# Tanh taken off by adding transfers instead of VectorE subtractions, in an fp32 attention and feed-forward kernel on Trainium2

## The chip, the cores and the metric

The kernel runs on one core of one Trainium2 chip. Five engines with queues of their own work side by side: TensorE (PE, with its weight loads shown apart as PEld), VectorE (DVE), ScalarE (ACT), GpSimd (POOL) and SyncE (SP). Each takes its instructions in the order in which they stand in its queue. Transfers are issued from SP's and POOL's queues and carried by 16 DMA engines. The time is the device's time of one execution in microseconds. The kernel before takes 674.85 us, the median of three runs (674.55 to 675.02).

## What is computed

The first part is a linear attention with a decay, over 4 batches, 8 heads, 768 positions and 64 channels. Its output, 3072 rows of 512, goes through a feed-forward part with 2048 hidden channels. All of it is float32.

```python
for b in range(nb):                       # blocks of 64 positions
    intra = np.einsum('bhic,bhjc->bhij', qb, kb) * Dmask[None]
    intra = np.einsum('bhij,bhjd->bhid', intra, vb)
    inter = np.einsum('bhid,bhde->bhie', qb * lam_pow[None], kv_state)
    out[:, :, sl] = intra + inter
    kv_state = lam_block[None, :, None, None] * kv_state + np.einsum('bhsd,bhse->bhde', kb_dec, vb)
...
h = x @ w_in                              # 3072x512 by 512x2048
g = h - np.tanh(h)
return (g @ w_out).astype(np.float32)     # 3072x2048 by 2048x512
```

## The kernel before

**Groups and units.** The rows are worked in six groups of 512 (`g` = 0 to 5), a group being 128 positions of each of the four batches. For a group the attention gives `xt`, 512 channels by 512 rows. The first product then makes the hidden blocks in four units (`u` = 0 to 3, 512 hidden channels each), and the second product makes the output rows out of them. Attention for group `g + 1` is run in pieces among the steps of group `g`.

**Seven products for eight.** From group 1 on, both products follow Strassen's scheme in Winograd's form: the operands are cut into quarters, seven products are made of sums of quarters, and their results are added into the four result blocks, called 11, 12, 21 and 22. `up(g, u, n)` (L424) issues product `n` of unit `u` of the first product; each is 8 matmuls of 128x256 in the trace. From group `GI` = 2 on, products 2 and 4 are themselves made in that way by `inner_steps` (L505), for all units at once and ahead of the rest, so that a unit is left with five: 6, 5, 1, 7 and 3. Product 1 of a unit is issued one unit early. Product 1, 6 and 7 gather in a PSUM bank y, products 5 and 3 in a bank z. There are two banks for y, which the units take in turn, and one for z: product 5 of a unit can't begin before VectorE has read z of the unit before.

**Result blocks.** `hidden(g, c)` (L418) is an SBUF tile for block `c` of all four units; there is one tile for each `c`, and the next group takes it over. After a product, `up` copies or adds its bank into these tiles: L446 adds y to block 11, L449 copies z to 22, L451 and L452 add y to 22 and 21, L461 copies y to 12, and L469 adds z to 12. `finish(c, src)` (L439) then takes the hyperbolic tangent off a block: ScalarE writes the tanh into a tile `th` (L441) and VectorE subtracts it from the block (L442). A block of a unit is 128 partitions by 512 float32, 256 KB. Behind the last of the four, L472 and L473 make two sums that the second product wants, S1 = 12 + 22 and then 12 = 11 - 12.

**Second product.** `down(g, 1)` reads block 11, `down(g, 2)` block 21; the others read 22, S1, 12 and differences made by `sums_once` (L626) and `sums_twice` (L676). Where a product of it is cut once more, `down_twice` (L684) issues it. The weight factors come from DRAM in pieces of 256 KB, in a fixed order, into a ring of seven tiles `wb` (`piece`, L594), issued from POOL. In group 2 the POOL queue also carries the making of the quarter factors: `load_quarters` (L571) loads them, `factors_twice` (L585) has VectorE make differences (L590) and stores them to DRAM (L591). Output tiles and some results between come from `otile` (L621), four buffers of 128x512 with the tag "o".

**Order.** The framework lays out each engine's queue: it takes the program's order as a priority and an estimate of when each instruction's inputs are ready, and puts in the semaphores. `keep_in_program_order` pins a few instructions. The loop that sets the order around the change:

```python
for n in (2, 6, 5, 7, 1, 4, 3) if g < GI else (1, 7, 3) if u == 0 else (6, 5, 1, 7, 3) if u + 1 < NU else (
        6, 5, 7, 1, 3):
    if n != 1:
        up(g, u, n)
    elif u + 1 < NU:
        up(g, u + 1, 1)
    else:
        every(down(g, 1))
```

The functions that the diff touches:

Of the kernel before, what the change touches and what calls it, by code (L numbers as in the profile page):

```python
# [13 lines left out]
AF = mybir.ActivationFunctionType  # L14
AL = mybir.AluOpType
# [8 lines left out]
def kernel(  # L24
# [32 lines left out]
    nc = tc.nc  # L57
# [8 lines left out]
    NU = DFF // 512  # L66
# [117 lines left out]
    GI = 2  # L184
# [224 lines left out]
    def product_bank(key, n):  # L409

        if n == 1:
            banks[key, "y"] = bank("y", "yb" if key[0] == "up" and key[2] % 2 else "ya", 1)
        if n in (2, 5):
            banks[key, "zw"[n == 2]] = bank("zw"[n == 2], "zw"[n == 2], 1)
        t = banks[key, {2: "w", 5: "z", 3: "z"}.get(n, "y")]
        return t.rearrange("q (m c) -> q m c", m=2), n in (1, 2, 5)

    def hidden(g, c):  # L418

        if (g, c) not in hid:  # L420
            hid[g, c] = gpool.tile([128, NU, 2, HB], F32, name=f"g{c}", tag=f"g{c}")
        return hid[g, c]

    def up(g, u, n):  # L424
        a, bname = FACT[n]
        wt = {"A11": w1[u][:, 0:2, 0], "A12": w1[u][:, 2:4, 0], "S3": w1[u][:, 0:2, 1], "A22": w1[u][:, 2:4, 1],
              "S1": ws[u][:, 0], "S2": ws[u][:, 1], "S4": ws[u][:, 2]}[a]
        x = xt[g][bname] if bname != "B11" else xt[g, 0][:, 0:2]
        key = ("up", g, u)
        t, first = product_bank(key, n)  # L430
        for m in range(2):
            for kt in range(2):
                nc.tensor.matmul(out=t[:, m, :], lhsT=wt[:, kt, ts(m, 128)], rhs=x[:, kt, :],  # L433
                                 start=first and m == 0 and kt == 0, stop=kt == 1, skip_group_check=True)

        def dst(c):
            return hidden(g, c)[:, u]

        def finish(c, src):  # L439
            th = work.tile([128, 2, HB], F32, name="th", tag="th")  # L440
            nc.scalar.activation(th, src, AF.Tanh)  # L441
            nc.vector.tensor_tensor(dst(c), src, th, op=AL.subtract)  # L442

        y, z, w = (banks[key, x].rearrange("q (m c) -> q m c", m=2) if (key, x) in banks else None for x in "yzw")
        if g >= GI and n == 1:
            nc.vector.tensor_tensor(dst(11), dst(11), y, op=AL.add)  # L446
            finish(11, dst(11))
        elif g >= GI and n == 5:
            nc.scalar.activation(dst(22), z, AF.Copy)  # L449
        elif g >= GI and n == 7:  # L450
            nc.vector.tensor_tensor(dst(22), dst(22), y, op=AL.add)  # L451
            nc.vector.tensor_tensor(dst(21), dst(21), y, op=AL.add)  # L452
            finish(22, dst(22))
            finish(21, dst(21))
        elif n == 1:
            nc.scalar.activation(dst(11), y, AF.Copy)
        elif n == 2:
            nc.vector.tensor_tensor(dst(11), dst(11), w, op=AL.add)
            finish(11, dst(11))
        elif n == 6:  # L460
            nc.scalar.activation(dst(12), y, AF.Copy)  # L461
        elif n == 7:
            nc.scalar.activation(dst(22), y, AF.Copy)
            nc.vector.tensor_tensor(dst(22), dst(22), z, op=AL.add)
            finish(22, dst(22))
        elif n == 4:
            finish(21, y)
        elif n == 3:
            nc.vector.tensor_tensor(dst(12), dst(12), z, op=AL.add)  # L469
            finish(12, dst(12))  # L470

            nc.vector.tensor_tensor(dst("S1"), dst(12), dst(22), op=AL.add)  # L472
            nc.vector.tensor_tensor(dst(12), dst(11), dst(12), op=AL.subtract)  # L473

# [144 lines left out]
    def otile(name):  # L621
        return opool.tile([128, 512], F32, name=name, tag="o")
# [219 lines left out]
    load_quarters(0)  # L842
    load_quarters(1)
    up(1, 0, 1)
    for g in range(1, NG):
        last = g == NG - 1
        p0, p1 = attention(g + 1) if not last else ([], [])
        for u in range(NU):
# [8 lines that stand above are left out]
                if g in turns:  # L857
                    made.append(n)
                    step = len(made) - turns[g][0]
                    for t, first in turns[g][1]:  # L860
                        if step == first:
                            if t > 1:
                                load_quarters(t)
                            making[t] = factors_twice(t)
                        if first <= step < first + 4:
                            next(making[t])
            if g == GI - 1:
                inner_weights(u)
            if not last and u > 1:
                run(p0[u - 2:u - 1])  # L870
# [65 lines left out]
```

## Time and profile before

| | |
|---|---|
| median of three runs | 674.85 us |
| span of the profiled execution | 672.3 us |
| granted TensorE clock | 1.00 throughout |
| stretch from 275 to 313 us (group 2, first product) | PE busy 37.46 us, DVE 32.36, ACT 12.80, POOL 14.24, DMA share 0.71 |
| stretch from 313 to 330 us (group 2, after it) | PE busy 17.00 us, DVE 17.00, POOL 5.54, DMA share 0.76 |
| tanh of a block (L441) | 630 ns on ScalarE |
| transfers issued from POOL | 541 to 757 ns on POOL each |
| software queue | 28976 packets, 96.49 MB, 45.4% of 16 engines' span |

The profile is of one execution. In its tables a line such as `L442 DVE TENSOR_TENSOR g<-g,th ... x76 | 51.9, 688 | 18.2` names line, engine, operation, what is written from what, and the count; then the busy time in us, the mean of one in ns, and the engine's idle time just before, with what ended it. In the timeline the first two columns are start and length in us, and a bracket holds the idle time before and its releaser. The stretches named by windows list busy time and count for each engine. In the rows of transfers the last number is the median time from issue to landing. The ends of matmuls are modelled, so starts are the better guide to TensorE's pace. A few matmul records can be missing from a trace.

### The profile page before, as it was taken

What the parts mean: (1) busy time and instruction counts of PE and PEld (TensorE: products, weight loads), DVE (VectorE), ACT (ScalarE), POOL (GpSimd) and SP (SyncE); (2) the same over time, 40 slices, a digit from 0 to 9 for tenths busy, and PEclk for the clock granted to TensorE, in tenths of its full rate; (3) what the DMA queues carried; (4) which work ended last, traced back from release to release, by engine and by line L of the source; (5) the groups of instructions that cost most, each with busy time, mean ns of one, the idle gap of its engine ahead of it and who ended that gap; (6) DMA issues with size and microseconds to landing.
All of it is one profiled execution on the core that took longest, in us unless ns stands there. A gap on an engine that the chain in (4) does not pass through costs nothing.

```text
span 672.3 us, 12869 instructions
## 1 busy us (share of the span) xinstructions
PE 661.7 (98%) x4824; PEld 576.3 (86%) x4824; DVE 481.3 (72%) x872; ACT 194.8 (29%) x373; POOL 200.5 (30%) x345
## 2 busy tenths in 40 slices
PE   8899999999999999999999999999999999999998
PEld 7688855558888999988999988899988899988997
DVE  4797867993887772499895379888358977357743
ACT  4564433423331111332112243112333112234110
POOL 0001424217332424244345201254300245400351
PEclk9999999999999999999999999999999999999999
DMA  9979799869855978587898632698730677610495
GB/s 209 222 205 236 238 268 255 290 147 271 249 148 139 243 191 210 127 239 236 228 285 253 176 80 58 150 292 255 225 73 13 160 236 220 217 35 1 126 289 164
DMA packets 162717, 128.80 MB, mean 192 GB/s; under 512 B 133856, under 2 KB 135008, under 8 KB 162656
## 3 DMA queue, kind: packets, MB, share of 16 engines
q0 software_dynamic: 28976, 96.49, 45.4%
q1 hardware_dynamic: 133536, 31.50, 23.6%
q8 instruction: 38, 0.62, 0.4%
q14 instruction: 23, 0.19, 0.1%
q10 hardware_dynamic: 144, 0.00, 0.0%
HBM read 103.55 MB, written 24.38 MB: 190 GB/s over the span
## 4 chain that ended last, share of the span: by engine, by line
PE 86%; issue 8%; DMA 2%; SPq 1%; POOL 1%; DVE 0%; ACT 0%; POOLq 0%; DVEq 0%; ACTq 0%
PE y L433 13%; PE y L695 11%; PE op L771 8%; PE z L433 8%; PE zw L695 8%; PE h L750 7%; PE w L642 4%; PE y L642 4%; PE y L517 4%; PE sp L327 3%; PE plain L642 3%; PE op L381 3%; PE z L517 2%; PE op L375 2%; PE kv L349 1%
## 5 line engine op out<-in xcount | busy, mean ns | idle before, releaser
L607 POOL DMA_DIRECT2D wb<-fine x147 | 79.4, 541 | 114.7 <-PE y L695 48.2
L610 POOL DMA_DIRECT2D wb<-factors x56 | 30.3, 543 | 155.2 <-PE y L642 97.3
L441 ACT ACTIVATE th<-g 128x512 f32<-128x512 f32 x76 | 47.6, 630 | 98.3 <-DVE g L446 33.2
L433 PE MATMUL y<-xt,w 128*128 128x256 f32 x320 | 74.0, 380 | 0.0
L433 PEld LDWEIGHTS y<-xt,w 128*128 128x128 f32 x320 | 59.9, 190 | 9.0 <-ACT g L521 0.9
L442 DVE TENSOR_TENSOR g<-g,th 128x512 f32<-128x512 f32 x76 | 51.9, 688 | 18.2 <-ACT th L441 18.1
L698 ACT ACTIVATE q<-y 128x128 f32<-128x128 f32 x84 | 23.3, 278 | 130.1 <-PE y L695 126.5
L750 PE MATMUL h<-xt,w 128*128 128x256 f32 x256 | 56.5, 381 | 2.0 <-DVE w L271 2.0
L771 PE MATMUL op<-wt,g 128*128 128x512 f32 x128 | 56.5, 595 | 0.0
L750 PEld LDWEIGHTS h<-xt,w 128*128 128x128 f32 x256 | 48.2, 190 | 9.2 <-DVE w L271 1.4
L695 PE MATMUL y<-wb,g 128*128 128x128 f32 x384 | 51.2, 278 | 0.0
L771 PEld LDWEIGHTS op<-wt,g 128*128 128x128 f32 x128 | 23.8, 190 | 27.7 <-issue 26.5
L695 PEld LDWEIGHTS y<-wb,g 128*128 128x128 f32 x384 | 46.4, 192 | 1.2 <-issue 0.3
L433 PE MATMUL z<-tt,ws 128*128 128x256 f32 x160 | 38.0, 380 | 0.0
L433 PE MATMUL z<-xt,ws 128*128 128x256 f32 x160 | 37.9, 380 | 0.0
L433 PE MATMUL y<-tt,ws 128*128 128x256 f32 x160 | 37.8, 379 | 0.0
L642 PE MATMUL y<-wb,g 128*128 128x256 f32 x160 | 35.6, 379 | 0.5 <-PE y L433 0.5
L198 POOL DMA_DIRECT2D raw<-in_moe_w_out_dram x16 | 8.9, 555 | 90.8 <-DVE g L758 52.3
L642 PE MATMUL w<-wb,g 128*128 128x256 f32 x160 | 35.8, 382 | 0.0
L331 DVE TENSOR_TENSOR ss<-sp,mask 128x512 f32<-128x512 f32 x48 | 30.9, 682 | 6.0 <-PE sp L327 6.0
L642 PEld LDWEIGHTS y<-wb,g 128*128 128x128 f32 x160 | 30.3, 190 | 5.0 <-PE y L433 0.9
L433 PEld LDWEIGHTS z<-xt,ws 128*128 128x128 f32 x160 | 30.3, 190 | 4.3 <-ACT g L449 0.2
(171 smaller groups left out, 1301.2 us busy)
## 6 DMA issues: line engine op xcount, KB each, us to landing
wb<-fine POOLq DMA_DIRECT2D x147, 256.0 KB, 3.9
wb<-factors POOLq DMA_DIRECT2D x68, 256.0 KB, 4.2
raw<-in_moe_w_out_dram POOLq DMA_DIRECT2D x16, 512.0 KB, 5.2
v_nat<-in_v_dram SPq DMA_DIRECT2D x24, 256.0 KB, 5.4
factors<-wt POOLq DMA_DIRECT2D x8, 768.0 KB, 5.0
wb<-fine_in POOLq DMA_DIRECT2D x24, 256.0 KB, 4.1
k_nat<-in_k_dram SPq DMA_DIRECT2D x20, 256.0 KB, 5.0
raw<-in_moe_w_in_dram SPq DMA_DIRECT2D x8, 512.0 KB, 5.9
```

Source lines behind the costliest of these rows:

```text
L331: tied(g == 0, nc.vector.tensor_tensor(ss[:, j], sp[j], mask[:, j], op=AL.mult))
L433: nc.tensor.matmul(out=t[:, m, :], lhsT=wt[:, kt, ts(m, 128)], rhs=x[:, kt, :], start=first and m == 0 and kt == 0, stop=kt == 1, skip_gro ...
L441: nc.scalar.activation(th, src, AF.Tanh)
L442: nc.vector.tensor_tensor(dst(c), src, th, op=AL.subtract)
L517: nc.tensor.matmul(out=dst[:, ts(u, 128)], lhsT=a, rhs=b, start=x in (1, 2, 5) and u == 0, stop=True, skip_group_check=True)
L607: nc.gpsimd.dma_start(out=t.rearrange("p m c -> p (m c)"), in_=fine[TWICE.index(n_), SUB.index(x_)].rearrange("p u c -> p (u c)"))
L610: nc.gpsimd.dma_start(out=t, in_=factors[XAT[FACT[n_][1]]][:, 2 * x_:2 * x_ + 2, :])
L642: nc.tensor.matmul(out=t[:, m, :], lhsT=a[:, u, kt, ts(m, 128)], rhs=wb[:, kt, :], start=first and u == 0 and m == 0 and kt == 0, stop=u = ...
L695: nc.tensor.matmul(out=dst, lhsT=a[:, u, :], rhs=wb[:, ts(u, 128)], start=x in (1, 2) and u == 0, stop=u == NU - 1, skip_group_check=True)
L698: nc.scalar.activation(keep, dst, AF.Copy)
L750: tied(u == 0, nc.tensor.matmul(out=hm[c][:, m, :], lhsT=w1[u][:, i, a, ts(m, 128)], rhs=xt[0, t][:, i, :], start=m == 0 and i == 0, stop= ...
L771: nc.tensor.matmul(out=obank[b], lhsT=g, rhs=wt[:, 2 * a:2 * a + 2, :], start=kt == 0 and a == 0, stop=kt == KH - 1 and a == 1)
```

## The change

From group 2 on, 13 of the 16 blocks of a group have their tanh taken off in another way: ScalarE computes tanh of the negated block, which is the negated tanh, into a tile of the four output buffers, and a transfer issued from POOL adds that tile onto the block in SBUF (`accum_op=add`). These are block 11 of all units, and blocks 22, 21 and 12 of units 0 to 2. Blocks 22, 21 and 12 of unit 3 keep the subtraction on VectorE. The two sums of a unit (L472, L473), which read the blocks 11, 12 and 22, are issued one unit later: those of unit `u - 1` behind product 3 of unit `u`, and those of unit 3 behind its own product 3. Groups 0 and 1 are as they were.

```diff
-        def finish(c, src):
+        def finish(c, src, by_dma=False):
+            if by_dma:
+                th = otile("nth").rearrange("q (m c) -> q m c", m=2)
+                nc.scalar.activation(th, src, AF.Tanh, scale=-1.0)
+                nc.gpsimd.dma_start(out=src, in_=th, accum_op=AL.add)
+                return
             th = work.tile([128, 2, HB], F32, name="th", tag="th")
             nc.scalar.activation(th, src, AF.Tanh)
             nc.vector.tensor_tensor(dst(c), src, th, op=AL.subtract)
 
+        early_unit = u + 1 < NU and g >= GI
+
+        def sums(u):
+            g11, g12, g22, s1 = (hidden(g, c)[:, u] for c in (11, 12, 22, "S1"))
+            nc.vector.tensor_tensor(s1, g12, g22, op=AL.add)
+            nc.vector.tensor_tensor(g12, g11, g12, op=AL.subtract)
+
...
         if g >= GI and n == 1:
             nc.vector.tensor_tensor(dst(11), dst(11), y, op=AL.add)
-            finish(11, dst(11))
+            finish(11, dst(11), True)
...
-            finish(22, dst(22))
-            finish(21, dst(21))
+            finish(22, dst(22), early_unit)
+            finish(21, dst(21), early_unit)
...
         elif n == 3:
             nc.vector.tensor_tensor(dst(12), dst(12), z, op=AL.add)
-            finish(12, dst(12))
-
-            nc.vector.tensor_tensor(dst("S1"), dst(12), dst(22), op=AL.add)
-            nc.vector.tensor_tensor(dst(12), dst(11), dst(12), op=AL.subtract)
+            finish(12, dst(12), early_unit)
+            if u > 0 and g >= GI:
+                sums(u - 1)
+            if not early_unit:
+                sums(u)
```

More of the change, by code (lines that the diff above doesn't have):

```diff
@@ L458, in up @@
             nc.vector.tensor_tensor(dst(11), dst(11), w, op=AL.add)
-            finish(11, dst(11))
+            finish(11, dst(11), early_unit)
         elif n == 6:
@@ L464, in up @@
             nc.vector.tensor_tensor(dst(22), dst(22), z, op=AL.add)
-            finish(22, dst(22))
+            finish(22, dst(22), early_unit)
         elif n == 4:
```

## The prediction

> **What bounds the kernel now.** I read the page first, then the four stretches in which the first product of a later group runs, then one unit of such a stretch instruction by instruction, then the DMA issues. The page:
>
> ```profile
> span 672.3 us, 12869 instructions
> PE 661.7 (98%) x4824; PEld 576.3 (86%) x4824; DVE 481.3 (72%) x872; ACT 194.8 (29%) x373; POOL 200.5 (30%) x345
> L442 DVE TENSOR_TENSOR g<-g,th 128x512 f32<-128x512 f32 x76 | 51.9, 688 | 18.2 <-ACT th L441 18.1
> wb<-fine POOLq DMA_DIRECT2D x147, 256.0 KB, 3.9
> fine<-wt POOLq DMA_DIRECT2D x12, 320.0 KB, 6.2
> ```
>
> PE is the bound. Its busy share alone does not prove that, so I took the starts of successive matmuls from the trace: a 128x256 one follows the last after 216 ns wherever nothing holds it. Against that pace, PE loses about 32 us in the whole run, most of it before 275 us or at changes of matmul form, which the change leaves alone. From 275 us on (groups 2 to 5, where the diff acts) two waits alone reach half a microsecond: 0.70 us at 303.6 and 1.13 us at 644.0. The first is PE waiting for the bank of y, which VectorE had still to read (L452), while the VectorE operations of the quarter factors (L590) stood in the same queue. The second is a load of the stream landing late, after the last changed unit. So whatever the change frees, about 0.7 us (0.1%) can be won directly.
>
> The windows of the first product, groups 3, 4 and 5 (columns: busy us and count on each engine, granted clock, DMA share, GB/s):
>
> ```profile
> 384.00:412.00 28.00, 28.00 (x133) 24.32 (x132) 20.21 (x32) 11.54 (x20) 0.00 (x0) 1.00 0.29 57
> 489.00:517.00 28.00, 28.00 (x132) 24.32 (x131) 20.27 (x32) 11.50 (x20) 0.54 (x1) 1.00 0.21 42
> 592.00:620.00 28.00, 28.00 (x133) 24.31 (x132) 19.54 (x30) 11.61 (x20) 0.00 (x0) 1.00 0.03 7
> ```
>
> VectorE is busy 20 of 28 us, POOL and the DMA engines almost idle. The change moves work from an engine that is not the bound to two idle ones. What matters is thus not load but the order in which things become ready. One unit of group 3:
>
> ```profile
> 398.26 1.89 PE L433 MATMUL y<-tt,ws 128*128 128x256 f32 x8
> 398.50 0.69 DVE L442 TENSOR_TENSOR g<-g,th 128x512 f32<-128x512 f32 x1 [0.16 <-ACT th L441]
> 399.11 0.68 DVE L469 TENSOR_TENSOR g<-g,z 128x512 f32<-128x512 f32 x1
> 399.88 0.63 ACT L441 ACTIVATE th<-g 128x512 f32<-128x512 f32 x1 [0.82 <-DVE g L469]
> 399.99 1.89 PE L433 MATMUL z<-tt,ws 128*128 128x256 f32 x8
> ...
> 401.27 0.69 DVE L472 TENSOR_TENSOR gS<-g,g 128x512 f32<-128x512 f32 x1
> 402.00 0.69 DVE L473 TENSOR_TENSOR g<-g,g 128x512 f32<-128x512 f32 x1
> 403.64 0.69 DVE L446 TENSOR_TENSOR g<-g,y 128x512 f32<-128x512 f32 x1 [0.95 <-PE y L433]
> 405.69 0.68 DVE L451 TENSOR_TENSOR g<-g,y 128x512 f32<-128x512 f32 x1
> 406.29 0.68 DVE L452 TENSOR_TENSOR g<-g,y 128x512 f32<-128x512 f32 x1
> ```
>
> A unit is five products of 8 matmuls, 5 x 8 x 216 ns = 8.63 us, and PE keeps that exactly. The one tight place is the bank z: L469 reads it at 399.11 to 399.79, and the fifth product of the next unit writes it from 399.99. z is complete about 0.2 us after 398.26 (the offset at which other readers follow a matmul's last), at 398.46. L469 may then start anywhere from 398.46 to about 399.1, which is 0.65 us of room. One unit later the two bounds are 407.09 and 407.74.
>
> **Part by part.** *Removed:* 13 of 16 subtractions in each of 4 groups, 52 x 0.688 = 35.8 us of VectorE. PE hides all of it except at 303.6, so it brings 0 to 0.7 us. *ScalarE:* the same 52 tanh of 0.63 us, 0.
>
> *Added on POOL:* 52 issues. Plain ones take 0.54 to 0.76 us, so 28 to 40 us, into 3 x 28 us holding 0.54 us of work and into group 2. Hidden in groups 3 to 5: the ring of second-product pieces is full there, with POOL waiting 29 to 32 us for PE. If that cover went, a load would be 0.54 us later per accumulation ahead of it.
>
> *Added on the DMA engines:* 13 transfers of 256 KB a group. The page gives the software queue 45.4% of 16 engines' span for 28976 packets, 168 ns each; 128 rows cost 128 x 168 / 16 = 1.35 us of all engines, perhaps twice that as the destination is read too. So 17.5 to 35 us a stretch, against 20 to 27 us free: hidden at the lower bound, queueing at the upper.
>
> *The landing of an accumulation* is in no row. From below: the 3.9 us of a plain load of this size, which as a copy leaves out fetching the destination. From above: 6.2 us, the slowest software rows, plus the engines' time of the two accumulations issued just before (2 x 1.35), so 8.9 us. A plain load and one more pass give 3.9 + 1.35 = 5.25; I take 5.7, between this and 6.2. The Trainium skill (DMA: Bandwidth & Descriptors, section on the anatomy of one software DMA) fits 2.0 us plus bytes over 436 GB/s, which for 256 KB is an estimate of 2.6 us. The trace's 3.9 us for a plain one disagrees; by the rule everything below would be hidden and the sum would be zero. The same page's section on issuing engines speaks against the change from the other side: every queue runs on the same 16 engines, so transfers issued from an idle POOL are not free where loads share them.
>
> *The moved sums.* The last block of a unit (12) is added at 399.11 now and at 398.46 at the earliest, when z is complete; 0.69 us of addition and 0.63 us of tanh, behind the two tanh before it on ScalarE, end near 399.85. Issue at 399.95; landing at 399.95 + 5.7 = 405.65. The two sums wait for it on VectorE's in-order queue. VectorE starts back-to-back operations 0.60 us apart. Behind the sums, if the queue's order puts them at the gap before L446 (where VectorE idles now), stand L446, L451, L452 and then the next L469: it starts at 405.65 + 5 x 0.60 = 408.65 instead of by 407.74, so PE waits 0.91 us for z. Behind L446 it is one operation less, 0.31 us. Behind L452 it is nothing. Which order the queue gets is not in the trace. The two harmful ones average 0.61 us. It can bite twice a group (the L469 of units 1 and 2; unit 3's z is not wanted soon), so 3 groups x 2 x 0.61 = 3.7 us.
>
> *Group 2.* There the POOL queue carries a chain of quarter loads and stores, the DMA share is 0.71 (window 275 to 313), and the pieces for the next product are issued at 296.8, 302.7 and 303.7, used at 307.6, 309.2 and 310.9. With a landing of 5 us the second has 1.5 us to spare. Some nine accumulations of 0.54 us or more precede it on POOL (4.9 us, half of it falling into POOL's present waits): 0 to 4 us lost, against 0 to 0.7 us and the faster L590 chain on VectorE won. I take 0.
>
> *Buffers.* The negated tanh take the four output buffers in turn. One comes round every 8.63 us; it is held 0.63 + 0.1 + 5.7 = 6.4 us. Covered up to a landing of 7.9 us; beyond it ScalarE waits, then its copies of y and z, then PE.
>
> *Two sums pushed past the last unit* add 1.2 us to a VectorE that is full from 313 to 330 us (17.0 of 17.0). Their readers (the products on S1, from about 335 us) come several microseconds later: 0; without that cover, 1.2 us a group.
>
> **Sum.** 672.3 + 3.7 + 0 = 676.0 us of span. The median stands 2.55 us above the span in the profile (launch and end): 674.85 + 3.7 = 678.5 us.
>
> **Rivals.** *Covered (0.34):* the sums stand behind L452, or the landing is below 4.8 us; then L469 is never late. For it: 8.63 us is one whole unit, and VectorE has six operations, 4.1 us, left in it. Against it: an idle in-order engine tends to be given the first work expected ready. Time 674.85 less 0 to 0.7, say 674.5. *Faster (0.13):* the wait at 303.6 goes, and shorter VectorE queues shift the order so that the late load at 644.0 goes too: 674.85 - 0.7 - 1.1 = 673.0. Against it: nothing in the diff touches that load. *DMA-bound (0.13, slower):* accumulations cost double and queue on the engines; from a landing of 7.9 us the buffers decide. At 8.9 us the z wait is 8.9 - 5.7 + 0.61 = 3.8 us at six places, 22.9 us, and 4 us in group 2: 701.7 us. Against it: DMA shares of 0.03 to 0.29. *Only group 2 (0.05, slower):* POOL's chain is delayed by half of its 4 us, 676.9 us.
>
> **How the numbers follow.** My forecast, the wait moved to VectorE's queue, has 0.35 and 678.5 us; its own range, landing 5.0 to 7.0 with either order, goes from 675 to 688. The whole range must reach the covered and faster cases below (673.5) and part of the DMA-bound case: 690, leaving some 2 in 10 outside. About 0.2% (1.35 us) is what tells a change of this kernel from none. Faster 0.13; same 0.34; slower 0.53 (0.35 + 0.13 + 0.05).
>
> **What would show it.** Right: in units 1 and 2 of groups 3 to 5, L469 idle on a landing or queued behind sums that waited for one, and PE's z matmuls released by L469 some 0.3 to 0.9 us late; landings of the new row near 5.7 us. Wrong: PE starts in these units still 216 ns apart (covered), or PE held by ScalarE (buffers), or lost time at 300 to 315 us alone (group 2). A landing under 4.8 us makes the forecast wrong at its root.

## The result and the profile after

The changed kernel takes 700.26 us, the median of four runs (699.75 to 703.23), beside 674.7 us for the kernel before on the same chip. The ratio is 1.0394, with a 95% interval from 1.0376 to 1.0412. It is slower by 25.6 us, as forecast in sign, and far outside the range. The profiled execution has a span of 698.0 us, 25.7 us more than before.

The page of the changed kernel, with the rows that answer to those shown above (L442 and L443 are now the negated tanh and its accumulating transfer, L453 and L454 the two sums, L458, L463, L464 and L481 the additions that were L446, L451, L452 and L469; further down, L473 is the copy of y that was L461, L603 and L614 the differences of the quarter factors and the loads of quarters that were L590 and L601, L713 an addition of the second product that was L700):

```profile
span 698.0 us, 12981 instructions
PE 668.3 (96%) x4824; PEld 578.0 (83%) x4824; DVE 447.8 (64%) x820; ACT 194.2 (28%) x373; POOL 246.0 (35%) x397
L443 POOL DMA_DIRECT2D g<-nth x52 | 48.3, 1121 | 67.5 <-ACT nth L442 66.6
L453 DVE TENSOR_TENSOR gS<-g,g 128x512 f32<-128x512 f32 x20 | 13.8, 689 | 68.0 <-DMA g<-nth 68.0
g<-nth POOLq DMA_DIRECT2D x52, 256.0 KB, 4.6
```

VectorE is busy 33.5 us less, near the 35.8 us announced. But it now stands 68.0 us in front of L453, the first of the two sums, with a landing (`DMA g<-nth`) as the releaser. That wait did not exist before. Whether it costs anything is read from PE, again from the starts of matmuls against their pace of 216 ns. The time that PE loses in the stretches of the first product, beyond that pace:

| | before | after | more |
|---|---|---|---|
| group 2 | 1.3 us | 11.1 us | 9.8 us |
| group 3 | 0.5 us | 6.3 us | 5.8 us |
| group 4 | 0.5 us | 5.6 us | 5.1 us |
| group 5 | 0.2 us | 2.9 us | 2.7 us |

These make 23.4 of the 25.7 us. Another 2.0 us is one wait at 666.9 us in group 5, for an addition of the second product (L713) at the end of VectorE's backlog:

```profile
666.87 1.16 PE L708 MATMUL zw<-wb,g 128*128 128x128 f32 x8 [1.84 <-DVE g L713]
```

One unit of group 3 in the timeline after:

```profile
407.31 1.89 PE L433 MATMUL z<-xt,ws 128*128 128x256 f32 x8
408.72 0.69 DVE L453 TENSOR_TENSOR gS<-g,g 128x512 f32<-128x512 f32 x1 [7.43 <-DMA g<-nth]
409.45 0.69 DVE L454 TENSOR_TENSOR g<-g,g 128x512 f32<-128x512 f32 x1
410.06 0.68 DVE L458 TENSOR_TENSOR g<-g,y 128x512 f32<-128x512 f32 x1
410.80 1.99 PE L433 MATMUL y<-tt,ws 128*128 128x256 f32 x8 [1.59 <-DVE g L458]
410.82 2.42 ACT L442 ACTIVATE nth<-g 128x512 f32<-128x512 f32 x4 [6.17 <-DVE g L458]
411.75 3.48 POOL L443 DMA_DIRECT2D g<-nth  x4 [8.52 <-ACT nth L442]
```

VectorE reached L453 early and stood there for 7.43 us. Behind it in the queue waited L458, which adds product 1 from the bank y to block 11. Product 6 of the unit accumulates onto the same bank, so PE may not start it until L458 has read the bank: PE's wait of 1.59 us names L458 as its releaser. The late L458 then lets four tanh go at once, four accumulations follow in one burst, and the fourth of them is the one that the next unit's sums wait for. This L453 and the next start 10.8 us apart (408.72 and 419.51), where a unit of PE's work is 8.63 us.

PE has eight waits of 0.5 us or more in groups 3 to 5. Six are of this kind, for the bank y. Two, at 425.16 and 535.45 us, are for the bank z; there operations of the attention (L306, L317) stand between L458 and L481 as well:

```profile
421.44 0.70 DVE L306 STREAM_TRANSPOSE qt<-q_blk 128x512 f32<-128x512 f32 x1
424.43 0.68 DVE L481 TENSOR_TENSOR g<-g,z 128x512 f32<-128x512 f32 x1
425.16 1.99 PE L433 MATMUL z<-tt,ws 128*128 128x256 f32 x8 [1.59 <-DVE g L481]
```

In group 2 the queue that holds things up is another one:

```profile
298.72 0.69 DVE L453 TENSOR_TENSOR gS<-g,g 128x512 f32<-128x512 f32 x1 [5.08 <-DMA g<-nth]
298.80 0.63 ACT L442 ACTIVATE nth<-g 128x512 f32<-128x512 f32 x1 [3.09 <-DMA g<-nth]
299.34 0.58 ACT L473 ACTIVATE g<-y 128x512 f32<-128x512 f32 x1
299.93 0.76 POOL L614 DMA_DIRECT2D wb<-factors  x1 [4.13 <-DMA fine<-wb]
299.97 3.58 PE L433 MATMUL y<-xt,w 128*128 128x256 f32 x8 [2.39 <-ACT g L473]
```

ScalarE waits for one of the four output buffers (its wait ends with a landing), and L473, the copy of y that PE needs, stands behind it. Three of the buffers are held because their accumulations are still to be issued: POOL stands 4.13 us in front of a quarter load whose ring slot is not free. The fourth is held by an accumulation that was issued at 288.36 us and landed 10.3 us later. Landings of accumulations in this stretch, taken one by one from the trace, are 4.5 to 10.3 us; the first of a burst in the units of group 3 takes 3.3 to 3.4 us.

The last line has a second loss in it: 8 matmuls take 3.58 us instead of 1.89. The windows there (columns: busy us and count of each engine, granted clock, DMA share, GB/s):

```profile
296.00:300.00 4.00, 1.61 (x9) 1.08 (x7) 1.25 (x2) 1.20 (x3) 0.07 (x1) 0.98 1.07 335
300.00:303.40 3.40, 3.40 (x9) 2.75 (x10) 1.47 (x4) 0.40 (x1) 3.40 (x6) 0.53 0.58 164
```

For 3.4 us after the wait, the granted clock is 0.53: matmuls start some 427 ns apart. It happens twice in group 2, and each time PE falls 1.7 us behind its pace. What that adds to the whole time is less certain: one of the four executions had a mean granted clock of 1.000 and took 700.28 us, no less than the profiled one (0.995, 699.75 us).

### The profile page after: what moved, and what is told of

It reads as the page before. It is cut to its first block, busy times and chain, and to the rows that moved or that the text cites. A ratio compares the mean times of both kernels' runs of the same rounds, so it can differ in the third digit from the quotient of the medians.

```text
span 698.0 us, 12981 instructions
## 1 busy us (share of the span) xinstructions
PE 668.3 (96%) x4824; PEld 578.0 (83%) x4824; DVE 447.8 (64%) x820; ACT 194.2 (28%) x373; POOL 246.0 (35%) x397
## 3 DMA queue, kind: packets, MB, share of 16 engines
q0 software_dynamic: 36464, 110.13, 55.2%
## 4 chain that ended last, share of the span: by engine, by line
PE 64%; issue 14%; DMA 9%; POOL 6%; DVE 3%; SPq 2%; ACT 1%; DVEq 0%; POOLq 0%; ACTq 0%
PE y L708 10%; PE op L784 8%; PE zw L708 8%; PE h L763 7%; PE y L433 5%; DMA g<-nth 5%; PE w L655 4%; PE y L655 4%; PE z L433 3%; POOL g L443 3%; PE sp L327 3%; PE op L381 2%; PE plain L655 2%; POOL wb L623 1%; DMA fine<-wb 1%
## 5 line engine op out<-in xcount | busy, mean ns | idle before, releaser
L433 PE MATMUL y<-xt,w 128*128 128x256 f32 x320 | 77.2, 393 | 5.6 <-ACT g L473 5.6
L433 PEld LDWEIGHTS y<-xt,w 128*128 128x128 f32 x320 | 61.8, 197 | 16.0 <-ACT g L473 6.4
L443 POOL DMA_DIRECT2D g<-nth x52 | 48.3, 1121 | 67.5 <-ACT nth L442 66.6
L453 DVE TENSOR_TENSOR gS<-g,g 128x512 f32<-128x512 f32 x20 | 13.8, 689 | 68.0 <-DMA g<-nth 68.0
L442 ACT ACTIVATE nth<-g 128x512 f32<-128x512 f32 x52 | 32.2, 630 | 80.2 <-DVE g L458 52.6
L623 POOL DMA_DIRECT2D wb<-factors x56 | 32.8, 594 | 60.8 <-PE y L655 15.7
L708 PEld LDWEIGHTS y<-wb,g 128*128 128x128 f32 x384 | 46.4, 192 | 1.3 <-issue 0.3
L433 PEld LDWEIGHTS y<-tt,ws 128*128 128x128 f32 x160 | 29.6, 190 | 14.3 <-DVE g L458 10.6
L433 PEld LDWEIGHTS z<-tt,ws 128*128 128x128 f32 x160 | 29.5, 190 | 9.9 <-DVE g L481 6.3
L655 PE MATMUL w<-wb,g 128*128 128x256 f32 x160 | 35.8, 382 | 0.0
L708 PE MATMUL zw<-wb,g 128*128 128x128 f32 x256 | 33.9, 275 | 1.8 <-DVE g L713 1.8
```

The lines of the kernel that those rows point to most:

```text
L442: nc.scalar.activation(th, src, AF.Tanh, scale=-1.0)
L443: nc.gpsimd.dma_start(out=src, in_=th, accum_op=AL.add)
L623: nc.gpsimd.dma_start(out=t, in_=factors[XAT[FACT[n_][1]]][:, 2 * x_:2 * x_ + 2, :])
L655: nc.tensor.matmul(out=t[:, m, :], lhsT=a[:, u, kt, ts(m, 128)], rhs=wb[:, kt, :], start=first and u == 0 and m == 0 and kt == 0, stop=u = ...
L708: nc.tensor.matmul(out=dst, lhsT=a[:, u, :], rhs=wb[:, ts(u, 128)], start=x in (1, 2) and u == 0, stop=u == NU - 1, skip_group_check=True)
```

## Experiments

Theory A: in groups 3 to 5 the loss is the place of the sums in VectorE's queue, ahead of L458. Rival B: the accumulations themselves cost, by load on POOL or on the DMA engines. For group 2 there were three candidates: the four buffers, POOL's order, and the load. Times are medians; ratios are to the kernel before on the same chip.

**Sums pinned.** `tied(yes, op)` pins an instruction behind the one that the program puts before it on its engine.

```diff
-            nc.vector.tensor_tensor(s1, g12, g22, op=AL.add)
+            tied(g >= GI, nc.vector.tensor_tensor(s1, g12, g22, op=AL.add))
```

> Kernel after the change, with the two sums of unit u-1 pinned on VectorE behind the addition of z (L481) of unit u, where the program has them; all 52 accumulations stay. Theory A (the wait for a landing stands in front of the additions that free the y bank: L453 waits, L458 is late, PE waits): the waits of 0.5 to 2.0 us in groups 3 to 5, 13.5 us in all, go; PE's starts there are 216 ns apart; group 2 keeps most of its 9.3 us; 685 to 689 us. Rival B (the accumulations themselves cost, by load on POOL or the DMA engines): little changes, 697 to 701 us.

684.75 us, ratio 1.0156 [1.0138, 1.0173]. PE's loss in groups 3, 4 and 5 is 0.4, 0.4 and 0.1 us, with every accumulation still there; group 2 loses 12.8 us, 1.7 us more than without the pin.

**Accumulations from group 3 on,** unpinned:

```diff
-        early_unit = u + 1 < NU and g >= GI
+        early_unit = u + 1 < NU and g >= GI + 1
...
-            finish(11, dst(11), True)
+            finish(11, dst(11), g >= GI + 1)
...
-            if u > 0 and g >= GI:
+            if u > 0 and g >= GI + 1:
```

> Kernel after the change, but group 2 subtracts on VectorE and makes its sums in the same unit, as before; groups 3 to 5 are as changed (39 accumulations). If group 2's loss is its own (POOL's queue of quarter factors and the four output buffers): 9 to 10.5 us less, 690 to 691 us, with the 13.5 us of groups 3 to 5 unchanged. If the loss of group 2 only moves on to group 3: 697 to 700 us.

689.77 us, 1.0221 [1.0195, 1.0247]. Group 2 loses 1.3 us, as before the change; groups 3 to 5 lose 5.9, 5.9 and 2.8 us. The two losses are separate.

**Both edits.**

> Both edits: accumulations from group 3 on, sums pinned. Theory A with a separate loss in group 2: within 1.5 us of the kernel before, 674 to 676.5 us, though 39 accumulations are left. Rival B: 688 to 691 us as with the first edit missing.

673.75 us, 0.9995 [0.998, 1.001]: no difference from the kernel before, with 39 accumulations in it. The same kind of unit as above, and the windows of the three stretches that were shown before:

```profile
406.56 1.89 PE L433 MATMUL y<-tt,ws 128*128 128x256 f32 x8
406.75 2.63 POOL L443 DMA_DIRECT2D g<-nth  x3 [0.90 <-ACT nth L442]
406.76 0.69 DVE L481 TENSOR_TENSOR g<-g,z 128x512 f32<-128x512 f32 x1 [0.37 <-PE z L433]
407.37 0.68 DVE L453 TENSOR_TENSOR gS<-g,g 128x512 f32<-128x512 f32 x1
```

```profile
384.00:412.00 28.00, 28.00 (x132) 24.50 (x131) 13.79 (x22) 11.71 (x19) 10.42 (x12) 1.00 0.93 163
489.00:517.00 28.00, 28.00 (x132) 24.51 (x131) 13.73 (x22) 11.72 (x19) 10.48 (x12) 1.00 0.87 146
592.00:620.00 28.00, 28.00 (x132) 24.52 (x131) 10.57 (x16) 11.75 (x20) 10.41 (x12) 1.00 0.66 114
```

L453 now follows L481 without a wait, and PE is never held. The DMA share has gone from 0.29, 0.21 and 0.03 to 0.93, 0.87 and 0.66, and that costs PE nothing here. Rival B is out for groups 3 to 5.

**Late sums alone.** Every tanh is subtracted on VectorE, and the sums stay one unit late.

```diff
         def finish(c, src, by_dma=False):
-            if by_dma:
+            if False:
```

> The sums one unit later as in the change, but every tanh taken off on VectorE as before: no accumulation at all. Theory A: nothing to wait for, 674 to 676 us. Rival C (the two sums pushed past the last unit cost by themselves in the full stretch of VectorE after it): 677 to 681 us.

673.71 us, 0.9999 [0.9985, 1.0012]. Pushing the two sums past the last unit costs nothing by itself.

**Sums behind L458, ahead of the rest** (accumulations from group 3 on, the sums pinned as above): the sums of unit u - 1 are made in the step of product 7.

```diff
         elif g >= GI and n == 7:
+            if u > 0 and g > GI:
+                sums(u - 1)
             nc.vector.tensor_tensor(dst(22), dst(22), y, op=AL.add)
...
-            if u > 0 and g >= GI + 1:
-                sums(u - 1)
```

> Accumulations from group 3 on, as in the run that came out even (673.75 us), but the sums of unit u-1 stand behind L458 (the addition of block 11) and in front of the two additions of product 7 and of L481. Theory A in its narrow form (the y bank, freed by L458, is what PE waits for): PE's waits for y go; what is left is z, freed by L481 behind sums that end some 0 to 1 us too late: 674 to 680 us. If any place ahead of L481 is as bad as the one in the change: 686 to 690 us, as with the same groups unpinned (689.8 us).

679.67 us, 1.0105 [1.0089, 1.0121]. The waits for y are gone; z waits remain, 0.5 and 2.5 us in group 3 and 0.5 us each in groups 4 and 5. This is the wait that the prediction priced: L453 waits for its landing (3.56 us), three more operations and L483, here the addition of z, follow, and PE's product 5 is late. Its 8 matmuls then run at half clock, 3.34 us.

```profile
408.50 0.69 DVE L453 TENSOR_TENSOR gS<-g,g 128x512 f32<-128x512 f32 x1 [3.56 <-DMA g<-nth]
411.03 0.68 DVE L483 TENSOR_TENSOR g<-g,z 128x512 f32<-128x512 f32 x1
411.77 3.34 PE L433 MATMUL z<-tt,ws 128*128 128x256 f32 x8 [2.37 <-DVE g L483]
```

**Block 12 alone accumulated,** from group 3 on, unpinned; blocks 11, 22 and 21 are subtracted.

```diff
-            finish(11, dst(11), g >= GI + 1)
+            finish(11, dst(11))
...
-            finish(22, dst(22), early_unit)
-            finish(21, dst(21), early_unit)
+            finish(22, dst(22))
+            finish(21, dst(21))
```

> Accumulations from group 3 on, sums not pinned (they stand ahead of L458 as in the change), but only block 12 of units 0 to 2 is accumulated, 9 in all; 11, 22 and 21 are subtracted on VectorE. The sums still wait in the queue for the same landing, but it is no longer the fourth of a burst. If it is the burst that makes the landing late: it lands 3.3 to 3.6 us after its issue, about 1.3 us ahead of the limit, and the time is that of the kernel before within 1.5 us. If any wait for a landing ahead of L458 costs: 680 to 690 us, as with all blocks of groups 3 to 5 (689.8 us).

682.78 us, 1.011 [1.0086, 1.0134]. The first expectation, the time of the kernel before, failed, although the landing mostly came as it said: 3.3 to 3.5 us after its issue in six of nine cases, 4.4 to 5.0 us in the others. The time lies in the range of the second, 680 to 690 us. The first left the subtractions out of account. They are back on VectorE and stand behind the waiting sum as well:

```profile
396.32 0.69 DVE L453 TENSOR_TENSOR gS<-g,g 128x512 f32<-128x512 f32 x1 [5.50 <-DMA g<-nth]
401.01 0.68 DVE L481 TENSOR_TENSOR g<-g,z 128x512 f32<-128x512 f32 x1
401.75 3.39 PE L433 MATMUL z<-tt,ws 128*128 128x256 f32 x8 [2.10 <-DVE g L481]
```

From L453 to L481 lie 4.7 us of queued work, where the preceding experiment has 2.5 us. So the burst alone does not set the price. What fits both runs is the landing plus all that VectorE has queued up to the next bank that PE wants.

**Plain copies in place of accumulations,** first in the changed kernel, then in the pinned one. A block is overwritten by its negated tanh; the difference from the block is left out.

```diff
-                nc.gpsimd.dma_start(out=src, in_=th, accum_op=AL.add)
+                nc.gpsimd.dma_start(out=src, in_=th)
```

> Kernel after the change with plain copies in place of accumulations: a block is overwritten by its negated tanh, and the difference from the block is left out. Same transfers, same waits. If the accumulation's own price (0.85 us on POOL against 0.54) makes the landings late: POOL 0.54 us each, the fourth of a burst lands 1.2 us sooner, waits of 2 us become 0.8, 690 to 694 us. If the order on VectorE decides and the price is small: 697 to 700 us. A time within 2 us of the kernel before would say that only accumulating costs.

678.13 us, 1.0075 [1.0059, 1.0092]. The sums still wait for landings (40.0 us in 12 places), but those come at a median of 3.4 us, and groups 3 to 5 lose 1.5, 1.3 and 0.1 us. None of the three expectations held: the price of accumulating matters more than its 0.3 us on POOL suggests. The reading that fits is that a landing that makes the limit costs nothing and one that misses it bunches the next; it was not tested by itself.

> The pinned kernel with all 52 transfers, as plain copies in place of accumulations (a block is overwritten by its negated tanh; the difference is left out). What is left of the loss there is group 2's 9.5 us and the half clock. If the accumulation's price on POOL and the DMA engines makes it (0.85 against 0.54 us, 1.5 against 0.6 us of all engines): 675 to 678 us. If the mere number of transfers among the quarter chain makes it: 681 to 685 us.

677.49 us, 1.0059 [1.0045, 1.0073]. Group 2 loses 4.9 us, against 12.8 us with accumulations in the same places. Most of its loss there is the price of accumulating, on POOL and in the landings:

```profile
L443 POOL DMA_DIRECT2D g<-nth x52 | 28.0, 541 | 63.6 <-ACT nth L442 57.8 <-ACT g L473 3.7 <-issue 1.4
```

**A fifth buffer** in the pinned kernel: block 11's negated tanh has a tile of its own.

```diff
-                th = otile("nth").rearrange("q (m c) -> q m c", m=2)
+                th = (late["pool"].tile([128, 512], F32, name="nth", tag="nth") if c == 11 else otile("nth")).rearrange("q (m c) -> q m c", m=2)
```

> The pinned kernel (684.75 us) with a fifth buffer: the negated tanh of block 11 has a tile of its own, those of 22, 21 and 12 go on sharing the four output buffers. What is left there is group 2's loss. Theory B (ScalarE waits for one of four buffers, its copies of y and z stand behind): the waits of PE for L473, 3.2 and 3.8 us, shrink by half or more, 677 to 681 us. Theory P (the accumulations stand on POOL's queue behind quarter loads that wait for a ring slot, so they land late whatever buffers there are): 682 to 686 us.

680.6 us, 1.0119 [1.0102, 1.0135]. Group 2 goes from 12.8 to 8.5 us. PE's waits for L473, 3.2 and 3.8 us, become none and 1.3 us; a wait of 3.1 us for L458 takes their place, which stands on VectorE behind an L603 that waits for a quarter load, and one of 1.5 us, at 319.6 us, is for a landing itself. So the buffers are one part and POOL's late loads another.

**Quarter chain on SP** in the pinned kernel: stores and quarter loads of group 2 go through SP, for the three factors made there.

```diff
-            nc.gpsimd.dma_start(out=fine[TWICE.index(MADE[t]), SUB.index(x)], in_=dst)
+            (nc.sync if t > 1 else nc.gpsimd).dma_start(out=fine[TWICE.index(MADE[t]), SUB.index(x)], in_=dst)
...
-                nc.gpsimd.dma_start(out=t.rearrange("p m (v c) -> p (m v) c", v=2),
+                nc.sync.dma_start(out=t.rearrange("p m (v c) -> p (m v) c", v=2),
```

> The pinned kernel with the stores of the quarter factors and the quarter loads of group 2 issued from SP in place of POOL; the same transfers, the same accumulations. Theory P: the accumulations no longer stand behind the 5.1 us wait for a ring slot, they land in 3.3 to 6 us, and group 2 loses less than 4 us: 675 to 679 us. Rival D (the DMA engines are full in group 2, share above 1.0, so everything lands late from whichever queue): 682 to 686 us.

716.55 us, 1.0663 [1.0636, 1.0691]; neither theory expected that. ScalarE's waits for a buffer fall to 1.6 us in two places, but one wait of 5.5 us is left in group 2, for an L458 behind an L603 that waits for a quarter load, and the chain now stands ahead of the attention's loads on SP: PE waits 6.0 us for a transposed block at 335 us, later 5.1 us for a piece of the stream and 5.1 us for a load of v. Around these waits the clock is granted at half for 34 us in all. Whether POOL's order alone would have kept the rest of group 2's loss stays open.

**Block 21 of group 2 added** to the kernel with both edits, which came out even (42 accumulations), and then **block 21 of group 2 alone** (3 accumulations, sums as before the change). The edits to `finish` of block 21:

```diff
-            finish(21, dst(21), early_unit)
+            finish(21, dst(21), u + 1 < NU)
```

```diff
-            finish(21, dst(21))
+            finish(21, dst(21), u + 1 < NU and g == GI)
```

> The kernel that came out even (accumulations from group 3 on, sums pinned), and in group 2 block 21 of units 0 to 2 accumulated as well, a block that no sum of the unit reads: 42 accumulations. If the wait of 0.7 us at 303 us is VectorE's backlog, three subtractions fewer shorten it: 672 to 674 us where the kernel before is 672.9 to 674.7, at most 0.1% faster. If three transfers among the quarter chain already hold POOL up: 675 to 678 us.

673.31 us, 0.9985 [0.9975, 0.9995]. PE's wait at 303 us falls from 0.7 to 0.3 us, but one of 0.3 us, for an addition of z, appears at 295.8 us.

> Kernel before, with one thing changed: in group 2, block 21 of units 0 to 2 is accumulated by a transfer (3 in all); all sums stay where they were. If the 39 accumulations of groups 3 to 5 give nothing because PE waits for nothing there, this is as fast as the run with 42 (ratio 0.9985 to the kernel before), 0.997 to 1.000, and PE's wait at 303 us is 0.3 us instead of 0.7. If the 42 owed their 0.15% to groups 3 to 5: 0.999 to 1.002.

673.88 us, 1.0003 [0.9994, 1.0012]. Only the second expectation's range, 0.999 to 1.002, holds it. The wait at 304.6 us is 1.2 us, released by a load of the stream. The 0.15% of the run above is thus not shown to come from these three accumulations, nor from the other 39, which by themselves gave 0.9995 [0.998, 1.001]. Its cause stays open.

## Why the prediction was wrong

**What bounds the kernel: right.** PE's pace is the same after. What was added are waits and, in the profiled execution, 6.8 us at half clock.

**The direct gain of at most 0.7 us: not contradicted.** The best version gained 0.15% (0.05 to 0.25%), some 0.3 to 1.7 us, and in its trace PE's waits in group 2 are hardly shorter in sum (0.3 and 0.3 us, for 0.7).

**The wait moved to VectorE's queue: right in kind, and this was the forecast.** Its price was wrong. The step that failed is the sum "3 groups x 2 x 0.61 = 3.7 us"; groups 3 to 5 lost 13.6 us. Three terms of it were off. First, it looked at the bank z alone ("the one tight place") and missed y: L446, behind the sums, must have read y before product 6 accumulates onto it, and that limit comes 1.73 us ahead of the one for z. With the step's own landing of 405.65, L446 would have ended at 407.54, after product 6's start at 406.89, so even its own numbers gave a wait at y. Second, it averaged two places in the queue, and the queue had the earlier one. Third, it held the units to be independent. A late L458 bunches the tanh, the bunch makes the landing of block 12 later (5.1 to 6.5 us after its issue where the sums of units 0 and 1 wait for it, and the issue itself moves), and eight places cost 0.5 to 2.0 us each, six at y and two at z, in place of 0.61 us at six, all at z.

**The landing of 5.7 us: right for the one that counts in groups 3 to 5.** Block 12, the fourth of a burst, landed after 5.1 to 6.5 us there. The bounds of 3.9 and 8.9 us did not hold for all: alone an accumulation landed in 3.3 us, in group 2 in up to 10.3 us. The row's median is 4.6 us, under the 4.8 us that the prediction named as the sign of being wrong; but the row mixes all blocks, and its median says nothing of block 12. The fit of the Trainium skill (DMA: Bandwidth & Descriptors, on the anatomy of one DMA) gives an estimate of 2.6 us for a plain transfer of this size; plain copies in these places landed in 2.3 us at best and 3.1 to 3.4 us in the median, and an accumulation in none of 52 cases under 3.3 us.

**Group 2, "I take 0": wrong.** This is the second step that failed: it lost 9.8 us, over twice its upper bound of 4. The step priced POOL's issues at 0.54 us and left the accumulations' landing at 5 us. On POOL an accumulation takes at least 0.85 us, and here it landed in 4.5 to 10.3 us, past the 7.9 us at which the prediction's own paragraph on buffers says that ScalarE waits. That paragraph was right, and the step on group 2 did not use it. The half clock, 3.4 of the 9.8 us in the profiled execution, was in no term. How the rest divides between the buffers, POOL's late loads and the landings is shown in part only: the fifth buffer took back 4.3 of the pinned kernel's 12.8 us, plain copies 7.9.

**POOL and the DMA engines as hidden cover in groups 3 to 5: right.** Shares up to 0.93 cost PE nothing once the sums were pinned. An accumulation took an estimated 1.54 us of all 16 engines ((55.2% x 698.0 less 45.4% x 672.3) / 52), inside the 1.35 to 2.7 us.

**The two sums past the last unit, 0:** right by themselves (the run with late sums alone); in the changed order VectorE's backlog did reach PE once, 2.0 us in group 5.

**The 2.55 us between span and median** are not launch and end alone. Each execution on record stands 1.7 to 1.9 us above its own span; the rest is that the profiled one was quicker than the median. The forecast of the difference does not depend on it.

**The rivals.** "Covered" is what happens once the order is pinned and group 2 left alone. The DMA-bound rival's 701.7 us is near the measured time by accident: it puts 22.9 us on z in groups 3 to 5 with landings of 8.9 us, and neither was so; only its remark that the buffers decide from 7.9 us came true, in group 2.

## What to carry to other kernels

Moving work from a busy engine to an idle one replaces a short local dependence by a transfer's latency, and an in-order queue passes that latency on to everything behind the first reader. So list, for each reader of the late result, what stands behind it in its queue and the nearest buffer that the bounding engine needs from any of it; check every such buffer, not the one that was tight before. If a scheduler lays out the queue by estimated readiness, pin the reader behind the work that must not wait: here that alone took back all of the loss in three groups of four, and none in the fourth, where other queues held things up.

## What the runs showed of the hardware

**An accumulating transfer costs far more than a copy.** For 256 KB within SBUF, the copy took 0.54 us on POOL, the accumulation 0.84 us at the least. By estimate the copy took 0.63 us of all 16 engines ((49.9% x 676.8 less 45.4% x 672.3) / 52), the accumulation 1.54 us. The queue counted 80 packets for a copy and 144 for an accumulation (33136 and 36464 in all, against 28976).

**The matmul clock halves after some waits, in pieces of 3.4 us.** It was granted at half for 3.41 us after waits of PE of 2.3 us (twice in the run with block 12 alone), 2.5 us (sums behind L458), 2.55 and 3.35 us (the changed kernel) and 3.1 us (five buffers), and for 6.83 us around one of 3.8 us (the pinned kernel). Waits of 2.6 us (accumulations from group 3 on) and 3.15 us (the pinned kernel) passed without it. So of two waits of like length one can put PE 1.7 us further behind. Executions of one kernel differ in it too: with block 12 alone, two with a mean clock of 1.000 took 680.11 and 681.68 us, two with 0.995 took 683.88 and 684.15 us; in the changed kernel the one with 1.000 was no quicker. The Trainium skill (TensorE: Matmul & The Clock Gate, Part 1) has the halving after an idle window of about 3.4 us that runs freely, and its table of goals advises against idle gaps over some 3 us; here 2.3 us was enough.
